# Block 0 of group 0 ahead of block 1's statistics, block 1's factors on GpSimd, and fewer dummy matmuls, in a fused state-space and MLP kernel

## The chip, the cores and the metric

The kernel runs on one core of a Trainium2 chip. The metric is the device time of one execution in microseconds (us). The kernel before took 154.12 us as the median of 3 runs (153.42 to 154.88). All times inside an execution are counted from the start of the profiled span.

## The reference, cut to what matters

One input x of 2048 tokens by 448 features is normalised, and two branches read the result: a linear recurrence over the tokens (A), and an MLP with a second normalisation (B). The output is x + A * silu(B).

```python
x = A_x
xn = _layernorm(x)
s = _A_ref(xn, ...)                    # h[t] = Lam_bar*h[t-1] + B_bar xn[t];  y = 2 Re(C h) + xn*Dskip
def _B_ref(x, w1, b1, w2, b2):
    y = _layernorm(x)
    h = _gelu(y @ w1 + b1)             # 448 -> 1792
    return h @ w2 + b2                 # 1792 -> 448
return x + s * _silu(_B_ref(xn, ...))
```

## The kernel before, in words

**Tiles.** The tokens are cut into four groups of 512, each group into two blocks (b = 0, 1) of 256, and each block into two halves (par = 0, 1: even and odd tokens) of 128. A half is one tile of 128 partitions by 448. For each group the MLP's first layer (mm1, L809) runs in seven steps j of two columns-of-128 each, every step in two phases: a first of 6 matmuls and a second of 8, then a GELU on ScalarE (L813). Then come the second layer (mm2, L836), and the recurrence's matmuls (L737, L879, L882).

**Order.** All work is a list of tasks. Each task names its engine and what it reads and writes, and the program adds semaphore waits for these dependences. The list ORDER (L162) gives the order in which tasks are issued, and so the order inside each engine's queue; SECOND (L181) lists the tasks that take the second of two possible engines. Every engine works strictly in its own order: what stands behind a waiting instruction waits too.

**The opening.** Group 0 starts differently from the others, because nothing is there yet. For block 0 each half is loaded on its own, for block 1 both halves come in one transfer. Per half there is a chain:

- `first_stats` (L424): BN_STATS and BN_AGGR on VectorE (L431, L432) give mean and variance, written `mv`; then the factor r1 = (var*(1+eps) + eps^2)^(-1/2). It is called r10, r12 for block 0's halves and r11, r13 for block 1's. It comes from ScalarE as Ln and Exp: for block 0 per half (L434, L435), for block 1 both halves together (L438, L439).
- `first_apply` (L447): VectorE writes the normalised half (L453; below `xm0p1`, `xm0p0`, `xm1p1`, `xm1p0` for block and half), TensorE transposes it in four pieces (L460), and ScalarE or VectorE copies the result to SBUF (L419; `xmT...`).
- mm1 of steps j = 0 to 4 for block 0 alone needs only block 0's two `xmT` tiles; j = 5, 6 run for both blocks, and j = 0 to 4 follow for block 1.

TensorE's order in the opening is: 26 dummy matmuls; `parameters` (L529, L530: five tiny matmuls that turn three parameter rows into columns); 12 dummies; transposes of xm0p1; 5 dummies; transposes of xm0p0; 5 dummies; `b1_columns` (L602, L603: six tiny matmuls that turn the bias b1 into columns, copied by L605 to `b1f`); 42 mm1 matmuls for j = 1, 2, 0 of block 0; the eight transposes of xm1p1 and xm1p0; then the other 126 mm1 matmuls, of which the first six are j = 4, the next 28 are j = 3, j = 4 and the first phase of j = 5, and the next 70 begin with j = 0 of block 1. A dummy (L422) multiplies the tile `ones`, which VectorE fills first (L309), into a bank that nobody reads.

Other tasks that matter below, all small: `ca` (L540, GpSimd) and `cr` (L541, ScalarE); `f2`, `f1`, `f4` on GpSimd (L534, L537, L552) and `f3` and a second `f2` on VectorE (L539, L538), where f4 reads f3; `iota` (L317, GpSimd); `ln_scale` (L478 to L482: five instructions on GpSimd, with a power in L480, that write all of group 0's factors again, among them the places of r10 to r13, so they must follow all readers of these); the three `wrap` instructions (L542 to L544, GpSimd) after it, and the Abs on ScalarE (L554) that reads their result. The table load for GELU (L443) is issued on ScalarE once cr and r10 to r13 are done. Copies of the upper 64 rows of w1 (L354, `w1c_0` to `w1c_3`, one for each chunk of w1) go on VectorE; a second phase of mm1 needs the copy of its chunk. The bias b1 comes in by two transfers that GpSimd issues (L363, L364).

Of the kernel before, what the change touches and what calls it, by code (L numbers as in the profile page):

```python
# [7 lines left out]
ACT = mybir.ActivationFunctionType  # L8
# [171 lines left out]
""".split()]  # L180
SECOND = [int(k) for k in """  # L181
46 54 55 62 64 67 70 75 77 84 108 113 131 134 159 161 163 164 166 178 185 186 188 190 191 221 223 225 227 229 231 239 249 250 259 267 269 332 363 365
366 385 401 402 437 448 469 481 483 488 492 500 502 503 505 511 529 530 610 613
# [8 lines left out]
LN_EPS = 1e-5  # L192
# [8 lines left out]
def bass_recurrent_scan__ssm_conv_s5__mixer_channel_mlp__prompt_kernel(  # L201
# [18 lines left out]
    with ExitStack() as es:  # L220
        def SB(name, shape, dtype=BF):
            return es.enter_context(nc.sbuf_tensor(name, shape, dtype))

        ident = SB("ident", [128, 128])
        ones = SB("ones", [128, 128])
# [80 lines left out]
        with nc.Block():  # L306

            S0 = -100
            dve(lambda e: e.memset(ones[:], 1.0), [], ["ones"])  # L309
# [110 lines left out]

            def dummies(n, rd=()):
                pe([lambda e: e.matmul(psum[:, 3, 0:128], ones[:, :], ones[:, :], start=True, stop=True) for _ in range(n)], ["ones", *rd], ["ps3"])  # L422

            def first_stats(b):  # L424

                for par in range(2):
                    q = 2 * par + b
                    var, mean = lnmv[:, 0, q, 1:2], lnmv[:, 0, q, 0:1]
                    r1, key = lnw[:, 0, 2, 1, q:q + 1], xk(0)[par:par + 1] if b == 0 else xk(1)
                    src, dst = x_all[:, b, par, :], xn2_sb[:, b, par * 512:par * 512 + D]  # L430
                    dve(lambda e, q=q, src=src: e.bn_stats(lnst[:, q, :], src), key, [f"st{q}"])  # L431
                    dve(lambda e, q=q: e.bn_aggr(lnmv[:, 0, q, :], lnst[:, q, :]), [f"st{q}"], [f"mv0_{q}"])  # L432
                    if b == 0:
                        kb.add("act", [lambda e, var=var, r1=r1: e.activation(r1, var, ACT.Ln, scale=1.0 + LN_EPS, bias=eps[:, 1:2]),  # L434
                                       lambda e, r1=r1: e.activation(r1, r1, ACT.Exp, scale=-0.5)], [f"mv0_{q}", "eps", "warm"], [f"r1{q}"], chain=True)  # L435
                    elif par == 1:
                        vs2, rs2 = lnmv[:, 0, 1:4:2, 1], lnw[:, 0, 2, 1, 1:4:2]
                        kb.add("act", [lambda e: e.activation(rs2, vs2, ACT.Ln, scale=1.0 + LN_EPS, bias=eps[:, 1:2]),  # L438
                                       lambda e: e.activation(rs2, rs2, ACT.Exp, scale=-0.5)], ["mv0_1", "mv0_3", "eps", "warm"], ["r11", "r13"], chain=True)  # L439

            def gelu_table():
                kb._sem("gelu0")
                kb.add("act", lambda e: e.preload_act_table_set("gelu_apprx_tanh_and_others"), ["cr", "r10", "r12"] + ["r11", "r13"] * (not 0), ["Wg0"], sem="gelu0")  # L443

            def first_apply(b):

                for par in range(2):  # L447
# [13 lines left out]
                    if b == 0:  # L461
                        if par == 0:
                            dummies(5, ["xm0p0"])
# [143 lines left out]

            def rows():

                for k, (dst, key, scale) in enumerate(((b2bc, "b2bc", 1.0), (dbc, "dbc", 0.5))):  # L610
                    bank, at = 6 - k, 64 + 32 * k
                    pe([lambda e, bank=bank, at=at: e.matmul(psum[:, bank, 0:D], ones[at:at + 1, :], vrows[at:at + 1, 64:512], start=True, stop=True)], ["ones", f"vr{3 + k}"], [f"ps{bank}"])
                    kb.either(("act", lambda e, bank=bank, dst=dst, scale=scale: e.activation(dst[:], psum[:, bank, 0:D], ACT.Copy, scale=scale)),
                              ("dve", lambda e, bank=bank, dst=dst, scale=scale: e.tensor_scalar(dst[:], psum[:, bank, 0:D], scale, None, op0=ALU.mult)), [f"ps{bank}"], [key])
# [309 lines left out]
            dummies(12 if 1 else 10, ["vr0"])  # L924
# [3 lines left out]
            dummies(5, ["st0"])  # L928
# [100 lines left out]
```

## Time and profile before

| what | value |
|---|---|
| median of 3 runs | 154.12 us (153.42 to 154.88) |
| the profiled execution's own time | 153.63 us |
| its span, first to last instruction | 151.9 us |
| TensorE (PE) busy | 147.6 us, 97% of the span, 1136 matmuls |
| VectorE (DVE), ScalarE (ACT), GpSimd (POOL) busy | 128.2, 98.4, 40.8 us |

The share of busy time says little about the opening, since TensorE counts as busy while it runs dummies. The opening is read from the rows in order of time, one engine after another. A row gives the start, the length, the engine, the line, the operation with what it writes and reads, the count of merged instructions and, in square brackets, how long the engine stood idle before and what ended that. "PEld" is the weight load that goes ahead of each matmul.

### The profile page before, as it was taken

What the parts mean: (1) busy time and instruction counts of PE and PEld (TensorE: products, weight loads), DVE (VectorE), ACT (ScalarE), POOL (GpSimd) and SP (SyncE); (2) the same over time, 40 slices, a digit from 0 to 9 for tenths busy, and PEclk for the clock granted to TensorE, in tenths of its full rate; (3) what the DMA queues carried; (4) which work ended last, traced back from release to release, by engine and by line L of the source; (5) the groups of instructions that cost most, each with busy time, mean ns of one, the idle gap of its engine ahead of it and who ended that gap; (6) DMA issues with size and microseconds to landing.
All of it is one profiled execution on the core that took longest, in us unless ns stands there. A gap on an engine that the chain in (4) does not pass through costs nothing.

```text
span 151.9 us, 2990 instructions
## 1 busy us (share of the span) xinstructions
PE 147.6 (97%) x1136; PEld 87.5 (58%) x1136; DVE 128.2 (84%) x270; ACT 98.4 (65%) x182; POOL 40.8 (27%) x100
## 2 busy tenths in 40 slices
PE   7999999999999999999999999999999999999992
PEld 7886755444566577545444556754444666555561
DVE  3978969899998969999999996379968727999984
ACT  3787998888789559997798610462579833067400
POOL 5377870053021910010366006200071040000200
PEclk9999999999999999999999999999999999999999
DMA  4999999889996100700003032610340001100022
GB/s 117 270 309 389 262 231 182 175 150 154 214 213 165 23 0 0 138 0 4 0 0 63 4 60 53 146 60 4 60 109 14 4 0 60 60 0 0 4 102 79
DMA packets 31236, 14.73 MB, mean 97 GB/s; under 512 B 24752, under 2 KB 30774, under 8 KB 31222
## 3 DMA queue, kind: packets, MB, share of 16 engines
q1 hardware_dynamic: 30912, 14.26, 41.9%
q0 software_dynamic: 160, 0.23, 0.6%
q8 instruction: 9, 0.15, 0.4%
q10 hardware_dynamic: 150, 0.05, 0.1%
q14 instruction: 5, 0.04, 0.1%
HBM read 6.89 MB, written 1.84 MB: 57 GB/s over the span
## 4 chain that ended last, share of the span: by engine, by line
PE 96%; DVE 2%; issue 0%; DVEq 0%
PE psum L809 29%; PE psum L836 28%; PE psum L737 14%; PE psum L879 12%; PE psum L882 4%; PE psum L422 3%; PE psum L720 3%; PE psum L885 1%; DVE t L893 1%; PE psum L460 1%; DVE tmp L899 1%; PE psum L705 1%; PE psum L602 0%; DVE ones L309 0%; PE psum L529 0%
## 5 line engine op out<-in xcount | busy, mean ns | idle before, releaser
L809 PE MATMUL psum<-xn2T,w_sb 64*128 64x512 bf16 (+1 forms) x462 | 44.6, 345 | 0.2
L836 PE MATMUL psum<-w_sb,gT 128*128 128x448 bf16 x224 | 44.4, 353 | 0.0
L813 ACT ACTIVATE gT<-psum,b1f 128x512 bf16<-128x512 f32 (+1 forms) x66 | 36.0, 625 | 10.6 <-PE psum L809 10.4
L809 PEld LDWEIGHTS psum<-xn2T,w_sb 64*128 64x128 bf16 x462 | 24.0, 109 | 19.7 <-ACT gT L813 2.3
L836 PEld LDWEIGHTS psum<-w_sb,gT 128*128 128x128 bf16 x224 | 21.6, 98 | 20.3 <-issue 0.6
L419 ACT ACTIVATE u_sb<-psum 128x512 bf16<-128x512 f32 (+2 forms) x22 | 10.5, 478 | 23.0 <-PE psum L737 22.7
L737 PE MATMUL psum<-xnT,BT 128*128 128x256 bf16 x196 | 24.0, 273 | 0.0
L737 PEld LDWEIGHTS psum<-xnT,BT 128*128 128x128 bf16 x196 | 18.9, 98 | 5.4 <-issue 1.1
L761 DVE TENSOR_TENSOR_SCAN s_w<-dk,vs 128x774 f32<-128x774 f32 x8 | 14.0, 1760 | 0.1
L899 POOL TENSOR_TENSOR tmp<-t,x_all 128x448 bf16<-128x448 bf16 x5 | 5.2, 1031 | 33.1 <-DVE t L896 30.7
L500 ACT ACTIVATE xn_sb<-x_all,lnw 128x448 bf16<-128x448 bf16 (+2 forms) x21 | 13.0, 661 | 1.2 <-DVE xn_sb L499 1.1
L419 ACT ACTIVATE vs<-s_w 64x256 bf16<-64x256 f32 (+2 forms) x16 | 10.9, 682 | 2.6 <-DVE s_w L761 1.5
L879 PE MATMUL psum<-CZ,h_sb 128*128 128x448 bf16 x56 | 11.9, 353 | 0.0
L839 DVE TENSOR_TENSOR o<-psum,b2bc 128x448 f32<-128x448 f32 x16 | 9.7, 614 | 1.7 <-PE psum L836 1.5
L879 PE MATMUL psum<-CQ,h_sb 128*128 128x448 bf16 (+2 forms) x54 | 10.5, 332 | 0.0
L879 PEld LDWEIGHTS psum<-CZ,h_sb 128*128 128x128 bf16 x56 | 5.4, 98 | 4.7 <-DVE lnmv L407 0.4
L401 DVE BATCH_NORM_STATS2 lnst<-x_all 128x6 f32<-128x448 bf16 x12 | 7.0, 614 | 0.6 <-DMA x_all<-in_A_x_dram 0.6
L879 PEld LDWEIGHTS psum<-CQ,h_sb 128*128 128x128 bf16 x54 | 5.1, 98 | 4.0 <-DVE t L893 0.4
L882 PE MATMUL psum<-M,xnT 128*128 128x448 bf16 x32 | 7.4, 352 | 0.0
L891 DVE TENSOR_TENSOR Cr<-psum,xd 128x448 f32<-128x448 f32 x7 | 4.3, 620 | 3.5 <-PE psum L885 3.4
L480 POOL TENSOR_TENSOR lnw<-lnw,mhalf 128x8 f32<-128x8 f32 x3 | 7.0, 2332 | 0.3
L499 DVE TENSOR_SCALAR xn_sb<-x_all,lnw 128x448 bf16<-128x448 bf16 (+2 forms) x19 | 6.9, 395 | 0.0
(160 smaller groups left out, 189.8 us busy)
## 6 DMA issues: line engine op xcount, KB each, us to landing
out_dram<-tmp SPq DMA_DIRECT2D x7, 224.0 KB, 2.0
x_all<-in_A_x_dram SPq DMA_DIRECT2D x3, 448.0 KB, 4.3
w_sb<-in_B_w_dram SPq DMA_DIRECT2D x3, 448.0 KB, 8.5
w_sb<-in_B_w_dram SPq DMA_DIRECT2D x3, 384.0 KB, 4.9
vs<-in_A_C_re_dram SPq DMA_DIRECT2D x1, 392.0 KB, 11.5
Bn<-in_A_B_im_dram SPq DMA_DIRECT2D x1, 336.0 KB, 10.4
Bn<-in_A_B_re_dram SPq DMA_DIRECT2D x1, 336.0 KB, 10.8
vs<-in_A_C_im_dram SPq DMA_DIRECT2D x1, 336.0 KB, 11.3
```

Of the source, the lines that this page charges most:

```text
L401: dve([lambda e, b=b, par=par, q=q: e.bn_stats(lnst[:, q, :], x_all[:, 2 * g + b, par, :])], [f"x{2 * g + b}"] , [f"st{q}"], 0.62, prio)
L419: kb.either(("act", [lambda e, o=o, i=i: e.activation(o, i, ACT.Copy) for o, i in pairs]), ("dve", [lambda e, o=o, i=i: e.tensor_copy(o, i ...
L480: power = fns + [lambda e: e.tensor_tensor(w(2), w(0), mhalf[:].to_broadcast([128, 2, nq]), ALU.pow), lambda e: e.tensor_tensor(w(3), mean ...
L500: ("act", [lambda e, o=o, i=i: e.activation(o, i, ACT.Identity, bias=nb, scale=rs) for o, i in parts], 0.75, 0.2)]
L737: fns = [lambda e, r=r, m=m, d=d: e.matmul(psum[:, 4, r * NK:(r + 1) * NK], BT[:, m, d, :], xnT[:, gx, d, :], start=(d == 0), stop=(d == 6 ...
L761: dve(lambda e, so=so, vi=vi: e.tensor_tensor_scan(so, dk[:].rearrange("p i c -> p (i c)"), vi, 0.0, ALU.mult, ALU.add), ["v", "vl", "dk", ...
L809: return lambda e: e.matmul(view(bk[k]), w1_sb[rows, d, fcol(2 * j + k)], rhs[rows, d, :, :], start=not second and n == 0, stop=second and ...
L813: act([lambda e, k=k: e.activation(gT[:, gb, 2 * j + k, :].rearrange("p (r c) -> p r c", r=2)[:, :, cols], view(bk[k]), ACT.Gelu_apprx_tan ...
L836: fns = [lambda e, fi=fi: e.matmul(psum[:, bk, 0:D], gT[:, gb, fi, q * 128:(q + 1) * 128], w2_sb[:, fi, :], start=(fi == 0), stop=(fi == N ...
L839: dve(lambda e: e.tensor_tensor(o2[:, fb, :], psum[:, bk, 0:D], b2bc[:], ALU.add), [f"ps{bk}", "b2bc"], [f"oo{fb}"], 0.62, prio - 76)
L879: fns = [lambda e, k=k: e.matmul(psum[:, bk, c0:c1], h_sb[:, hb, k, k0:k0 + 128], cm[:, k, c0:c1], start=(k == 0), stop=False) for k in ra ...
L882: fns += [lambda e, d=d: e.matmul(psum[:, bk, c0:c1], xnT[:, gx, d, xs], M0[:, d, c0:c1], start=False, stop=(d == 3)) for d in range(4)]
```

## The change

The diff, with ORDER and SECOND left out (they are renumbered, since the task that filled `ones` is gone):

```diff
-        ones = SB("ones", [128, 128])
...
-            dve(lambda e: e.memset(ones[:], 1.0), [], ["ones"])
...
+            one = nc.const_aps.tensor_like(1.0, ident[:])
+
             def dummies(n, rd=()):
-                pe([lambda e: e.matmul(psum[:, 3, 0:128], ones[:, :], ones[:, :], start=True, stop=True) for _ in range(n)], ["ones", *rd], ["ps3"])
+                pe([lambda e: e.matmul(psum[:, 3, 0:128], one, one, start=True, stop=True) for _ in range(n)], list(rd), ["ps3"])
...
-                        kb.add("act", [lambda e: e.activation(rs2, vs2, ACT.Ln, scale=1.0 + LN_EPS, bias=eps[:, 1:2]),
-                                       lambda e: e.activation(rs2, rs2, ACT.Exp, scale=-0.5)], ["mv0_1", "mv0_3", "eps", "warm"], ["r11", "r13"], chain=True)
+                        kb.add("pool", [lambda e: e.tensor_scalar(rs2, vs2, 1.0 + LN_EPS, LN_EPS * LN_EPS, op0=ALU.mult, op1=ALU.add),
+                                        lambda e: e.tensor_tensor(rs2, rs2, mhalf[:, 0, :].to_broadcast([128, 2]), ALU.pow)], ["mv0_1", "mv0_3", "mhalf"], ["r11", "r13"], chain=True)
...
-                kb.add("act", lambda e: e.preload_act_table_set("gelu_apprx_tanh_and_others"), ["cr", "r10", "r12"] + ["r11", "r13"] * (not 0), ["Wg0"], sem="gelu0")
+                kb.add("act", lambda e: e.preload_act_table_set("gelu_apprx_tanh_and_others"), ["cr", "r10", "r12"], ["Wg0"], sem="gelu0")
...
-                            dummies(5, ["xm0p0"])
+                            dummies(2, ["xm0p0"])
...
-            def rows():
...
-            dummies(12 if 1 else 10, ["vr0"])
+            dummies(9, ["vr0"])
...
-            dummies(5, ["st0"])
+            dummies(3, ["st0"])
```

`rows` was never called. The dummies now read a constant 1.0 that the runtime's preamble has already stored, one element for each partition, read 128 times over. Apart from the renumbering, ORDER and SECOND move these tasks, and no others:

| engine | order before | order after |
|---|---|---|
| TensorE | xm0p0's transposes, dummies, b1_columns, mm1 | xm0p0's transposes, b1_columns, dummies, mm1 |
| VectorE | ones, ..., xm0p1, stats of block 1 half 0, xm0p0, stats of half 1, both aggregates, copy xmT0p0, w1c_1, b1f, w1c_0, f3, f2, xm1p1, xm1p0 | ..., xm0p1, xm0p0, stats of block 1 half 0, copy xmT0p0, b1f, stats of half 1, both aggregates, w1c_0, f3, f2, xm1p1, xm1p0 |
| ScalarE | copy xmT0p1, cr, block 1's factors, table load | copy xmT0p1, cr, w1c_1, table load |
| GpSimd | ident, eps, eps, ident, b1 transfer 1, mhalf, b1 transfer 2, ca, iota, f2, ..., sgn, f1, f4, ln_scale, wrap | ident, b1 transfer 1, b1 transfer 2, ident, eps, eps, mhalf, ca, f2, f1, f4, iota, block 1's factors, ..., sgn, ln_scale, wrap |

The order of transfers on SyncE's queue is the same.

More of the change, by code (lines that the diff above doesn't have):

```diff
@@ L162 @@
 ORDER = [int(k) for k in """
[17 rows of a table removed]
[17 rows of a table added]
 """.split()]
 SECOND = [int(k) for k in """
-46 54 55 62 64 67 70 75 77 84 108 113 131 134 159 161 163 164 166 178 185 186 188 190 191 221 223 225 227 229 231 239 249 250 259 267 269 332 363 365
-366 385 401 402 437 448 469 481 483 488 492 500 502 503 505 511 529 530 610 613
+28 45 53 54 61 63 66 69 74 76 83 107 112 130 133 158 160 162 163 165 177 184 185 187 189 190 220 222 224 226 228 230 238 248 249 258 266 268 331 362
+364 365 384 400 401 436 447 468 480 482 487 491 499 501 502 504 510 528 529 609 612
 """.split()]
@@ L606, in b1_columns @@
                           ["ps4"], ["b1f"])
-            def rows():
[L610 to L614, printed above, removed]
             def skips():
```

34 rows, old and new, of the table ORDER are left out of this document.

## The prediction

> **What bounds the kernel now.** I read the busy times by stretch first, then the chain that ended last, then the rows in order of time of each engine from 1 to 17 us.
>
> ```profile
> PE 147.6 (97%) x1136; PEld 87.5 (58%) x1136; DVE 128.2 (84%) x270; ACT 98.4 (65%) x182; POOL 40.8 (27%) x100
> ...
> 12.50:19.40 6.90, 6.77 (x95) 4.66 (x94) 6.52 (x26) 6.27 (x14) 5.35 (x19) 1.00 1.09 311
> 19.40:147.50 128.10, 128.10 (x881) 71.88 (x882) 111.25 (x211) 83.89 (x149) 28.45 (x57) 1.00 0.36 71
> ```
>
> The columns of the last two are the stretch, its length, then busy time and count of PE, PEld, DVE, ACT, POOL. From 19.40 to 147.50 TensorE is busy in 128.10 of 128.10 us. So what the change makes earlier or later up to 19.4 us, it makes so for the end. TensorE's own rows of the opening:
>
> ```profile
> 1.11 2.95 PE L422 MATMUL psum<-ones 128*128 128x128 bf16 x26 [1.11 <-DVE ones L309]
> ...
> 4.30 1.46 PE L422 MATMUL psum<-ones 128*128 128x128 bf16 x12
> 5.56 0.50 PE L460 MATMUL psum<-ident,xn_sb 128*128 128x128 bf16 x4
> 5.89 0.44 PE L422 MATMUL psum<-ones 128*128 128x128 bf16 x5
> 6.17 0.39 PE L460 MATMUL psum<-ident,xn_sb 128*128 128x128 bf16 x4
> ...
> 7.17 2.48 PE L809 MATMUL psum<-xn2T,w_sb 64*128 64x256 bf16 x42
> 9.58 0.62 PE L460 MATMUL psum<-ident,xn_sb 128*128 128x128 bf16 x8
> 10.14 9.25 PE L809 MATMUL psum<-xn2T,w_sb 64*128 64x256 bf16 x126
> ...
> 10.58 1.57 PEld L809 LDWEIGHTS psum<-xn2T,w_sb 64*128 64x128 bf16 x28 [0.20 <-ACT gT L813]
> 12.47 4.94 PEld L809 LDWEIGHTS psum<-xn2T,w_sb 64*128 64x128 bf16 x70 [0.32 <-ACT gT L813]
> ```
>
> Real work starts at 7.17. The 12 dummies run to 5.56, and the transposes of block 0 stand behind them; block 1's transposes are at 9.58, directly behind the 42 matmuls, without a wait. The two waits for ACT show that GELU is nearly as binding here as TensorE. VectorE's and ScalarE's rows:
>
> ```profile
> 4.44 0.40 DVE L453 TENSOR_SCALAR xn_sb<-x_all,lnmv,lnw 128x448 bf16<-128x448 bf16 x1
> ...
> 5.58 0.62 DVE L431 BATCH_NORM_STATS2 lnst<-x_all 128x6 f32<-128x448 bf16 x1
> 6.12 0.30 DVE L432 BATCH_NORM_AGGREGATE lnmv<-lnst 128x2 f32<-128x6 f32 x2
> 6.60 0.42 DVE L419 COPY xn2T<-psum 128x512 bf16<-128x512 bf16 x1 [0.17 <-PE psum L460]
> 7.05 0.29 DVE L354 COPY w_sb<-w_sb 64x512 bf16<-64x512 bf16 x1
> 7.26 0.16 DVE L605 COPY b1f<-psum 128x14 f32<-128x14 f32 x1
> 7.34 0.22 DVE L354 COPY w_sb<-w_sb 64x256 bf16<-64x256 bf16 x1
> 7.59 0.17 DVE L539 TENSOR_SCALAR ang<-ang 128x4 f32<-128x4 f32 x1
> ...
> 7.74 0.70 DVE L453 TENSOR_SCALAR xn_sb<-x_all,lnmv,lnw 128x448 bf16<-128x448 bf16 x2
> 9.31 0.31 DVE L354 COPY w_sb<-w_sb 64x512 bf16<-64x512 bf16 x1 [0.88 <-DMA w_sb<-in_B_w_dram]
> ...
> 10.19 0.75 DVE L419 COPY xn2T<-psum 128x512 bf16<-128x512 bf16 x2
> ...
> 4.88 0.20 ACT L435 ACTIVATE lnw<-lnw 128x1 f32<-128x1 f32 x1
> ...
> 6.09 0.60 ACT L419 ACTIVATE xn2T<-psum 128x512 bf16<-128x512 bf16 x1 [0.70 <-PE psum L460]
> ...
> 7.28 1.28 ACT L443 ACT_TABLE_LOAD   x1
> 8.65 0.84 ACT L813 ACTIVATE gT<-psum,b1f 128x256 bf16<-128x256 f32 x2
> 9.69 1.57 ACT L813 ACTIVATE gT<-psum,b1f 128x256 bf16<-128x256 f32 x4 [0.20 <-PE psum L809]
> ...
> 13.03 0.23 ACT L554 ACTIVATE ang<-ang 128x16 f32<-128x16 f32 x1
> 13.89 3.94 ACT L813 ACTIVATE gT<-psum,b1f 128x512 bf16<-128x512 f32 x8 [0.63 <-PE psum L809]
> ```
>
> Block 1 is normalised at 7.74 to 8.44, so it has 1.1 us in hand before TensorE asks for it at 9.58. This slack is what the change spends.
>
> **The change, part by part.**
>
> *The fill of `ones` and the first dummies.* VectorE's fill, for which TensorE waited until 1.11, goes, and the 26 dummies start up to 0.25 us sooner (an estimate: VectorE's fill and its hand-over). Parameters behind them may still wait for their rows' transfer. I take no gain here; if nothing else holds them, all up to 5.56 moves by 0.25. A repeated element as operand is in no row: between nothing and 0.05 us for each of 14 dummies, 0.7 in all; the first 26 hide theirs. I take nothing, since the operand has the same shape. `rows` was never called: nothing.
>
> *Fewer dummies.* The 12 start (1.46 - 0.31)/11 = 0.105 apart, 0.31 being the length of one. Nine end at 4.30 + 9 x 0.105 = 5.25, 0.31 sooner. xm0p1 is ready (4.44 + 0.40 = 4.84). xm0p0 now follows it at once: r10 is ready at 4.88 + 0.20 = 5.08, so it runs 5.11 to 5.49. The four transposes take 0.42 at that pace, to 5.67, the three dummies to 5.89 (later ones stand 0.056 apart), and xm0p0's transposes begin at 5.89 instead of 6.17. Before, the copy began 0.43 after that and mm1 0.57 after the copy: now the copy is at 6.32 and mm1 at 6.89, 0.28 sooner. VectorE is free for it: block 1's first statistics end at 5.40 + 0.62 = 6.02. b1_columns come ahead of the last dummies; their transfers are issued earlier on GpSimd, past eps and ident; these are first wanted by block 0's factors and by parameters, which stand right ahead of the 12 dummies of 4.30, so I cost this at nothing (if it held parameters, all would move with them one for one).
>
> *ScalarE.* Its two small operations for block 1 go, w1c_1 comes in (0.6 by the row of the same width at 6.09, against 0.29 on VectorE). Copy of xmT0p1 at 5.88 to 6.48, cr, w1c_1 to about 7.1, table load 7.12 instead of 7.28, first GELU 8.49 instead of 8.65. mm1 wants w1c_1 after twelve matmuls, at 7.6: covered. The third pair's GELU follows TensorE: 9.41 instead of 9.69.
>
> *Block 1's statistics, now behind block 0.* From the copy at 6.32, by the spacings of the rows: b1f +0.45 (6.60 to 7.05) at 6.77; statistics of half 1 +0.08 at 6.85; both aggregates done +0.84 (5.58 to 6.42) at 7.69. Before it was 6.42. Then w1c_0 at 7.61, and f3 +0.25 at 7.86, done 8.03.
>
> *The factors on GpSimd.* Its rows:
>
> ```profile
> 5.68 0.34 POOL L317 IOTA dk<- 128x256 f32 x1
> 6.12 0.23 POOL L534 TENSOR_SCALAR cw<-cw 128x4 f32<-128x4 f32 x1
> ...
> 7.85 0.39 POOL L552 TENSOR_SCALAR ang<-ang 128x8 f32<-128x8 f32 x1 [1.14 <-DVE cw L538]
> 8.72 0.20 POOL L478 TENSOR_SCALAR lnw<-lnmv 128x4 f32<-128x4 f32 x1 [0.48 <-ACT L443]
> 9.00 0.19 POOL L479 TENSOR_SCALAR lnw<-lnmv 128x4 f32<-128x4 f32 x1
> 9.28 1.68 POOL L480 TENSOR_TENSOR lnw<-lnw,mhalf 128x8 f32<-128x8 f32 x1
> ...
> 12.47 0.22 POOL L544 TENSOR_TENSOR ang<-ang 128x16 f32<-128x16 f32 x1
> ```
>
> In the new order f4 and iota stand ahead of the factors, and f4 waits for f3 on VectorE. That is the new wait: f4 starts 0.09 after f3 (7.76 to 7.85), at 8.12 to 8.51; iota at 8.46; the next instruction 0.44 after it (5.68 to 6.12) at 8.90; the power 0.28 later (8.72 to 9.00) at 9.18. Its price for 2 columns is not in the trace: between 0.19 (a plain instruction) and 1.68 (the power of 8 columns, if it is all fixed cost). I take 0.19 fixed plus 2/8 of the other 1.49, 0.57, since a power that costs far more than a plain instruction of the same tile should go with its elements. So the factors are there at 9.75, against about 7.2 before.
>
> *Who waits.* VectorE waits at xm1p1 until 9.84; xm1p1 and xm1p0 take 0.70, to 10.54, and w1c_2, two table instructions and the copies of block 1's transposes (10.19 before) stand behind. TensorE is through its 42 at 6.89 + 2.48 = 9.37, and waits: first transposes at 10.28, the second four at 10.58, each 0.28 long, done 10.86. The next six mm1 matmuls start there, against 10.14: 0.72 late, the 0.28 won included. The 28 after them start at 11.19, against 10.58 (there ACT held them by 0.20): 0.61 late. They need the copies of block 1 only for their last six, at 12.3, when VectorE has done them (about 12.2). So 70 matmuls start at 13.08 against 12.47: 0.61 late.
>
> *ln_scale and the Abs.* ln_scale overwrites the factors, so it waits for xm1p0: 10.63 instead of 8.72, 1.91 late. The wrap ended at 12.69 and now ends at 14.60; the Abs stands on ScalarE ahead of the GELU of 13.89, which then starts at 14.88. TensorE would let it start at 13.89 + 0.61 = 14.50: it is 0.38 late. Its cover:
>
> ```profile
> 15.83 1.63 ACT L813 ACTIVATE gT<-psum,b1f 128x512 bf16<-128x512 f32 x3
> ...
> 15.74 1.48 PE L809 MATMUL psum<-xn2T,w_sb 64*128 64x256 bf16 x24
> ```
>
> The fifth GELU begins at 15.83, so the fourth frees its bank there; TensorE, at 15.74, comes to that bank after six matmuls of 0.055, at 16.07. With some 0.1 for the semaphore this leaves 0.15. So TensorE loses 0.38 - 0.15 = 0.23 more. The b2 transfer on GpSimd's queue moves behind ln_scale too; its first reader stands behind the first mm2, so I cost it at nothing (without that cover it would add 1.91 at most).
>
> *Sum.* 0.61 + 0.23 = 0.84 us later at 19.4, and so at the end. The profiled execution took 153.63 (span 151.9 and 1.73 around it): 154.47. The median shown is 0.49 above that execution, which makes it 154.96, say 155.0.
>
> **The rivals.**
>
> *ScalarE sets the pace, and the opening's gain stays (the other side).* If the factors come in time, the GELU that runs 0.28 sooner pulls everything: 154.12 - 0.28 = 153.8. It decides at the factors' time: the six matmuls must be done when GELU frees their bank at 10.2, so block 1's transposes by 9.9 and the factors by 8.8. For it: TensorE waited for ACT twice, and if the first dummies start 0.25 sooner, all moves by that, and the power may cost 0.19. Against it: both together bring 9.75 to 9.12 only; f4's wait for f3 would have to shorten too.
>
> *The power has a fixed cost.* At 1.68 for 2 columns everything behind it is 1.11 later: 0.84 + 1.11 = 1.95, 156.1. For it: other instructions on GpSimd cost nearly the same for 4 and for 8 columns (0.23 and 0.39). Against: only the power is so dear.
>
> *TensorE stays slow.* The dummies stand 0.105 apart up to 5.56 and 0.056 after 5.89, though the clock column shows 1.00 throughout; full pace came some 4.6 us after the first matmul. With idle stretches in the opening it may come later. If it came another 4.6 us later, at 10.3, the 42 matmuls would do in 3.4 us what takes 1.7, and end at 11.1; the wait for block 1 hides most of it, and 0.8 remains: 155.8. Against: it came while dummies, parameters and transposes were mixed, and of 48 dummies 40 remain.
>
> [...]
>
> **How the numbers follow.** Forecast 0.55; ScalarE's pace 0.18; power with fixed cost 0.15; slow TensorE 0.08; something else 0.04. The range takes in the case on the other side with the scatter of runs (153.5) and the dear power (156.2). The likeliest case alone spans 154.4 (power 0.19, and half of the Abs) to 155.7 (operands of dummies dear, ln_scale's power longer). A measurement of this kernel tells about 1% from no change: 152.6 and 155.7 are the bounds. Slower by over 1%: 0.15, half of the slow case, and 0.08 of the forecast's upper end, 0.27. Faster by over 1% has no mechanism here, since the opening has at most 0.5 us to give: 0.04. Within 1%: 0.69.
>
> **What would show it.** Right: mm1's first row at about 6.9; f4 on GpSimd ending its wait for f3 near 8.1; the power at 9.2 and about 0.6 long; a gap of TensorE of some 0.9 ahead of block 1's transposes; the Abs ahead of a GELU near 14.9; mm2 starting 0.8 after 19.32. Wrong: block 1's transposes directly behind the 42 matmuls (then the time falls), the power at over 1 us, 42 matmuls that take 4 us, or a start of mm2 that is later while the end is not.

## The result, and the profile after

| | median | shortest to longest | executions |
|---|---|---|---|
| before, in this comparison | 153.77 us | 153.3 to 154.88 | 4 |
| changed | 155.75 us | 155.41 to 156.22 | 4 |

The ratio is 1.0128, with a 95% interval from 1.0089 to 1.0166. The changed kernel is slower, by 1.98 us; 0.84 was forecast, and slower by over 1% had a chance of 0.27. A ratio, here and below, leaves out executions over 1.5% above the kernel's fastest: 1 of 12 in two of the experiments and 4 of 11 in the last one. Its profiled execution took 155.45 us, with a span of 153.7, 1.8 longer than before's 151.9. TensorE's rows of it first (start, length, engine, line, operation; the bracket is idle time ahead of the row and what ended it). mm1 is line 801 now and mm2 line 828:

```profile
4.20 0.70 PE L422 MATMUL psum<-const-bfloat16-1.0 128*128 128x128 bf16 x9
5.29 0.40 PE L460 MATMUL psum<-ident,xn_sb 128*128 128x128 bf16 x4 [0.40 <-DVE xn_sb L453]
...
7.06 4.12 PE L801 MATMUL psum<-xn2T,w_sb 64*128 64x256 bf16 x42
11.12 0.62 PE L460 MATMUL psum<-ident,xn_sb 128*128 128x128 bf16 x8
...
20.86 1.31 PE L828 MATMUL psum<-w_sb,gT 128*128 128x448 bf16 x6
```

mm2 starts at 20.86 against 19.32, so 1.54 of the 1.8 us are lost by then. But there is no wait ahead of block 1's eight transposes. Instead the 42 matmuls of block 0 took 4.12 us; before they took 2.48. The stretches show why (stretch, length, busy time and count of PE, PEld, DVE, ACT, POOL, then the granted clock of TensorE, the DMA share and GB/s):

```profile
5.80:7.20 1.40, 1.10 (x16) 0.78 (x16) 1.40 (x5) 1.15 (x4) 0.63 (x3) 0.95 0.85 219
7.20:10.20 3.00, 3.00 (x30) 2.55 (x29) 1.25 (x7) 2.16 (x4) 1.68 (x6) 0.50 1.05 307
10.20:12.50 2.30, 2.30 (x38) 1.74 (x34) 2.21 (x8) 1.34 (x5) 1.63 (x3) 0.94 1.06 362
```

The granted clock is 0.50 from 7.20 to 10.20. Finer stretches of the same profile read 1.00 up to 7.06, 0.54 from 7.06 to 7.20, 0.50 from 10.20 to 10.48 and 0.98 from 10.48 to 10.60, so the half clock lasted from about 7.06 to 10.48. That is the rival "TensorE stays slow", in another form: the dummies had reached full pace (nine in 0.70 from 4.20), and then the granted clock fell to 0.50. TensorE's longest stop before that, 0.40 us ahead of 5.29, came of a late transfer: VectorE waited 0.54 us for the second half of block 0, as it does in neither of the two later profiles of this kernel.

```profile
4.11 0.63 DVE L431 BATCH_NORM_STATS2 lnst<-x_all 128x6 f32<-128x448 bf16 x1 [0.54 <-DMA x_all<-in_A_x_dram]
```

Whether this stop let the clock fall was not tested. The new chain on GpSimd is there too, but block 1 was ready before TensorE asked:

```profile
8.24 0.24 POOL L552 TENSOR_SCALAR ang<-ang 128x8 f32<-128x8 f32 x1 [1.52 <-DVE cw L538]
8.44 0.35 POOL L315 IOTA dk<- 128x256 f32 x1
8.87 0.19 POOL L438 TENSOR_SCALAR lnw<-lnmv 128x2 f32<-128x2 f32 x1
9.14 0.73 POOL L439 TENSOR_TENSOR lnw<-lnw,mhalf 128x2 f32<-128x2 f32 x1
```

f4 (L552) waits 1.52 us for f3, which stands right ahead of the L538 that the row names; iota and the factors stand behind it, as forecast. The power takes 0.73. One execution thus shows a wait that is hidden and a clock that is not the usual one. It could not say what the change costs typically, nor through what. So the changed kernel was profiled again, twice.

### The profile page after: what moved, and what is told of

Its sections match the earlier page's. It is cut to its first block, busy times and chain, and to the rows that moved or that the text cites. A ratio compares the mean times of both kernels' runs of the same rounds, so it can differ in the third digit from the quotient of the medians.

```text
span 153.7 us, 2974 instructions
## 1 busy us (share of the span) xinstructions
PE 148.6 (97%) x1128; PEld 87.6 (57%) x1128; DVE 128.3 (83%) x268; ACT 98.6 (64%) x181; POOL 41.9 (27%) x102
## 3 DMA queue, kind: packets, MB, share of 16 engines
HBM read 6.89 MB, written 1.84 MB: 57 GB/s over the span
## 4 chain that ended last, share of the span: by engine, by line
PE 89%; DVE 3%; ACT 3%; DMA 2%; issue 1%; SPq 0%; DVEq 0%; ACTq 0%
PE psum L828 28%; PE psum L801 26%; PE psum L729 14%; PE psum L871 12%; PE psum L874 4%; PE psum L712 3%; DMA x_all<-in_A_x_dram 2%; ACT gT L805 2%; PE psum L877 1%; ACT L618 1%; DVE t L885 1%; DVE lnst L431 1%; DVE tmp L891 1%; PE psum L697 1%; DVE o L831 0%
## 5 line engine op out<-in xcount | busy, mean ns | idle before, releaser
L801 PE MATMUL psum<-xn2T,w_sb 64*128 64x512 bf16 (+1 forms) x462 | 46.2, 355 | 0.6 <-ACT gT L805 0.3
L801 PEld LDWEIGHTS psum<-xn2T,w_sb 64*128 64x128 bf16 x462 | 25.2, 112 | 20.7 <-ACT gT L805 2.9
L480 POOL TENSOR_TENSOR lnw<-lnw,mhalf 128x8 f32<-128x8 f32 x3 | 7.0, 2332 | 0.3
```

Source lines behind the costliest of these rows:

```text
L801: return lambda e: e.matmul(view(bk[k]), w1_sb[rows, d, fcol(2 * j + k)], rhs[rows, d, :, :], start=not second and n == 0, stop=second and ...
```

## The experiments

The theory to be tested is the prediction's: the factors come late on GpSimd, and TensorE waits for block 1. The first rival is the clock, that is, too few dummies. Each run is compared with before, run on the same chip; the number behind a time is the ratio to it with its 95% interval.

### The changed kernel again, unchanged, twice

> The changed kernel once more, unchanged, for more executions beside a second profile. Theory F (block 1's factors are late because they stand behind f4's wait for f3): TensorE waits some 0.7 to 1.0 us ahead of block 1's transposes when its pace is full, and the time is 1.0 to 1.5 above the kernel before, in every execution. Theory C (half clock decides): the 42 matmuls take about 4.1 us again and the transposes stand directly behind them; in executions without the half clock the time is near that of the kernel before, so the times fall into two groups 1.5 us apart.

It took 154.69 us (1.0066, 1.0045 to 1.0088), 0.92 above before, a little less than was expected of the wait; one execution of nine (155.87) lies apart. This is TensorE in its profiled execution (154.44, span 152.6), in three stretches of time:

```profile
6.62 2.50 PE L801 MATMUL psum<-xn2T,w_sb 64*128 64x256 bf16 x42
9.94 0.70 PE L460 MATMUL psum<-ident,xn_sb 128*128 128x128 bf16 x8 [0.82 <-DVE xn_sb L453]
10.57 2.63 PE L801 MATMUL psum<-xn2T,w_sb 64*128 64x256 bf16 x38
...
19.73 2.44 PE L828 MATMUL psum<-w_sb,gT 128*128 128x448 bf16 x12
...
30.43 5.36 PE L801 MATMUL psum<-xn2T,w_sb 64*128 64x512 bf16 x48
36.09 4.12 PE L801 MATMUL psum<-xn2T,w_sb 64*128 64x512 bf16 x36 [0.30 <-ACT gT L805]
```

At full pace the 42 matmuls end at 9.12 and TensorE waits 0.82 us for VectorE's xn_sb. This is the forecast's gap. VectorE in turn waits for the factors, which GpSimd has done at 8.72 + 0.73 = 9.45:

```profile
8.72 0.73 POOL L439 TENSOR_TENSOR lnw<-lnw,mhalf 128x2 f32<-128x2 f32 x1
9.48 0.70 DVE L453 TENSOR_SCALAR xn_sb<-x_all,lnmv,lnw 128x448 bf16<-128x448 bf16 x2 [1.70 <-POOL lnw L439]
```

A third measurement asked which of the first two is the usual one:

> The changed kernel, unchanged. Theory (wait, gap at the table load, and half the clock in some executions): near 154.7, and a median over 155.3 only if the 42 matmuls of block 0 take over 3 us in its profile. Rival (the first measurement's 155.75 is the typical one, the second's 154.69 was not): 155.5 or more with the 42 at 2.5.

154.69 us again (1.0073, 1.0044 to 1.0102), with the 42 matmuls in 2.50 and a wait of 0.69. So the usual cost of the change is 0.9 to 1.0 us, and the wait is in both of these profiles. Of all 22 executions of the changed kernel 7 took over 155.2 us: all 4 of the first measurement, 1 of 9 and 2 of 9 of the others.

### The dummies put back

```diff
-                            dummies(2, ["xm0p0"])
+                            dummies(5, ["xm0p0"])
-            dummies(9, ["vr0"])
+            dummies(12, ["vr0"])
-            dummies(3, ["st0"])
+            dummies(5, ["st0"])
```

> The changed kernel with 12, 5 and 5 dummies again instead of 9, 3 and 2; all else as changed. Theory A (the clock: idle stretches of TensorE in the opening let it fall to half pace from about 7 to 10 us): the 42 matmuls take 2.5 us instead of 4.1, and block 1's transposes then wait for their factors until about 10.4 instead of starting at 11.1, so the time falls by about 0.7 us against the changed kernel, to about 155.0, and stays 1.2 above the kernel before. Theory B (the factors alone): no change against the changed kernel, 155.7. If the slow pace came by chance of the run and not of the dummies, the mean does not move either.

154.66 us (1.0064, 1.0039 to 1.009), the same as the changed kernel's usual time. That is below both forecasts, which took the first measurement's 155.75 for the usual time. More dummies don't bring the loss back, so the usual loss isn't the clock. Its profiled execution was its longest (155.59) and shows a cost that I had put at nothing:

```profile
10.71 0.70 PE L460 MATMUL psum<-ident,xn_sb 128*128 128x128 bf16 x8 [0.65 <-DVE xn_sb L453]
...
28.92 2.82 PE L828 MATMUL psum<-w_sb,gT 128*128 128x448 bf16 x14 [0.31 <-DVE o L831]
```

Here mm1 began at 7.56, so everything behind it was later. The b2 transfer, issued at 15.83, took 8.5 us to land (7.4 from 15.07 in the changed kernel's second profile), and TensorE waited 0.31 us for `o`, which wants b2.

### Block 1's factors ahead of f4 and iota

One task is moved up in ORDER: 101 are the factors, 65 is iota.

```diff
-28 30 100 114 23 54 57 5 101 65 32 53 ...
+28 30 100 101 114 23 54 57 5 65 32 53 ...
```

> The changed kernel with block 1's factors ahead of f4 and iota on GpSimd, so that they no longer wait for f3 on VectorE. Theory A: block 1 is ready at about 9.6 instead of 10.6, but TensorE is at half pace until about 10 and comes to the transposes at 11.1 anyway; gain at the opening 0, and at most 0.3 later through ln_scale and the b2 transfer, which move up by 1 us: 155.4 to 155.7. Theory B: the transposes follow at 9.6 and the time falls by 0.9 or more, to 154.8 or less.

153.71 us (0.9992, 0.997 to 1.0013): with this one move the loss is gone. The factors wait for their own statistics only, and TensorE for nothing ahead of block 1's transposes (GpSimd's rows, then TensorE's):

```profile
7.27 0.22 POOL L438 TENSOR_SCALAR lnw<-lnmv 128x2 f32<-128x2 f32 x1 [1.07 <-DVE lnmv L432]
7.57 0.73 POOL L439 TENSOR_TENSOR lnw<-lnw,mhalf 128x2 f32<-128x2 f32 x1
```

```profile
6.54 2.50 PE L801 MATMUL psum<-xn2T,w_sb 64*128 64x256 bf16 x42
8.98 0.62 PE L460 MATMUL psum<-ident,xn_sb 128*128 128x128 bf16 x8
...
35.26 4.77 PE L801 MATMUL psum<-xn2T,w_sb 64*128 64x512 bf16 x42 [0.29 <-ACT gT L805]
```

That shows the theory: it is the place behind f4's wait that costs, not the engine on which the power runs. But mm2 starts at 18.91, 0.41 before before's 19.32, while the span (151.8) is only 0.1 shorter. Some 0.3 is given back, in the last row's wait near 35, which before doesn't have. It comes from ScalarE, behind the last silu (L833):

```profile
30.44 0.58 ACT L833 ACTIVATE g_sb<-o 128x448 bf16<-128x448 f32 x1 [0.59 <-DVE o L831]
31.41 1.28 ACT L618 ACT_TABLE_LOAD   x1 [0.39 <-ACT g_sb L833]
```

The same two rows of before:

```profile
30.85 0.58 ACT L841 ACTIVATE g_sb<-o 128x448 bf16<-128x448 f32 x1 [1.04 <-DVE o L839]
31.51 1.28 ACT L626 ACT_TABLE_LOAD   x1
```

The table load for group 1's GELU came 0.08 us after the silu's end before, and comes 0.39 after it now. Every profile of the changed kernel has this, on ScalarE and on TensorE.

### Only the dummies, and both undone

> The kernel before with 9, 3 and 2 dummies instead of 12, 5 and 5; nothing else. Theory A: the pace falls here too, the 42 matmuls take up to 1.6 us longer, and the time rises by 1 to 1.6 us, to 154.8 to 155.4. Theory B: fewer dummies only bring mm1 forward, by 0.1 to 0.3 us: 153.5 to 153.8.

The kernel before with 9, 3 and 2 dummies: 153.6 us (0.9991, 0.997 to 1.0011). In its profile mm1 starts at 6.82 instead of 7.17, the 42 matmuls take 2.62 us, and the granted clock is 1.00 throughout from 4.00 to 19.40. Fewer dummies alone neither cost nor bring anything that this measurement can tell.

> The changed kernel with 12, 5 and 5 dummies and with the factors ahead of f4 and iota. Theory A: with full pace and the factors at about 8.8, mm1 starts near 7.2 and nothing waits long: within 0.3 us of the kernel before, 153.5 to 154.1. Theory B: the same as with the factors ahead alone, 154.8 or less, since dummies play no part.

The changed kernel with the dummies put back and the factors moved: 153.84 us (1.0015, 0.9994 to 1.0036). Again no loss. The dummies put back alone took 154.66 on the same chip; the two kernels differ in the one move, which is thus worth 0.82.

### The factors on ScalarE

```diff
-                        kb.add("pool", [lambda e: e.tensor_scalar(rs2, vs2, 1.0 + LN_EPS, LN_EPS * LN_EPS, op0=ALU.mult, op1=ALU.add),
-                                        lambda e: e.tensor_tensor(rs2, rs2, mhalf[:, 0, :].to_broadcast([128, 2]), ALU.pow)], ["mv0_1", "mv0_3", "mhalf"], ["r11", "r13"], chain=True)
+                        kb.add("act", [lambda e: e.activation(rs2, vs2, ACT.Ln, scale=1.0 + LN_EPS, bias=eps[:, 1:2]),
+                                       lambda e: e.activation(rs2, rs2, ACT.Exp, scale=-0.5)], ["mv0_1", "mv0_3", "eps", "warm"], ["r11", "r13"], chain=True)
```

> The changed kernel with block 1's factors on ScalarE as Ln and Exp again, ahead of the table load in ScalarE's order; all else as changed. Theory F: block 1's transposes follow the 42 matmuls without a wait (factors at about 8.3), but the table load now ends near 9.6 and the third pair's GELU near 11.3, so TensorE waits there instead and the 70 matmuls start about 0.8 us later than in the kernel before: 154.6 to 155.0, and the move to GpSimd is worth something only if the wait for f3 goes. Theory C: no difference to the changed kernel, 155.7.

154.11 us (1.0024, 1.0008 to 1.004). The wait ahead of the transposes goes; they start at 9.21. But the factors hold the table load, which now begins at 8.00, and TensorE waits behind the transposes instead:

```profile
9.21 0.62 PE L460 MATMUL psum<-ident,xn_sb 128*128 128x128 bf16 x8
10.36 2.82 PE L801 MATMUL psum<-xn2T,w_sb 64*128 64x256 bf16 x36 [0.53 <-ACT gT L805]
```

mm2 starts at 19.74, as late as in the changed kernel's second profile (19.73): with the statistics behind block 0's normalising, the factors cost the opening as much on ScalarE as on GpSimd behind f4. Only the place ahead of f4 made the move off ScalarE worth while (18.91 there). The time is below the expected 154.6 to 155.0: the 70 matmuls start 0.42 later than before (12.89), not 0.8, and the loss at the second table load is missing. That load stands 0.07 behind its silu here, without the gap. The page of the changed kernel counts 181 instructions on ScalarE:

```profile
PE 148.6 (97%) x1128; PEld 87.6 (57%) x1128; DVE 128.3 (83%) x268; ACT 98.6 (64%) x181; POOL 41.9 (27%) x102
```

The page of before has 182, and that of this kernel 183. That made a theory of the 0.3: it hangs on the place of the table load in ScalarE's stream of instructions.

### One more instruction on ScalarE

A copy of 128x1 into a spare tile, behind the first table load, which nothing reads:

```diff
-            act(lambda e: e.preload_act_table_set("natural_log_exp_and_others"), [], ["warm"], 0.05, 5 * PINNED, "exp")
+            act([lambda e: e.preload_act_table_set("natural_log_exp_and_others"), lambda e: e.activation(spare[:], nc.const_aps.tensor_like(1.0, spare[:]), ACT.Copy)], [], ["warm"], 0.05, 5 * PINNED, "exp")
```

First together with the moved factors:

> The changed kernel with the factors ahead of f4 and iota, and one small spare ScalarE copy (128x1) right behind the first table load, whose result nobody reads. It puts every later ScalarE instruction one place further in the stream, where it stood in the kernel before. Theory P (the 0.39 us ahead of the second GELU table load, 0.08 in the kernel before, hangs on the place in ScalarE's instruction stream): the gap is 0.08 again, TensorE does not wait for GELU ahead of group 1's third pair, and the time falls by 0.3 us against the factors ahead alone, to about 153.4. Theory Q (it hangs on when the last silu is done): the gap stays 0.39, 153.7.

153.35 us (0.9986, 0.9957 to 1.0016), the shortest median of all, though the interval takes in no change. The gap is gone, on ScalarE and on TensorE:

```profile
30.45 0.58 ACT L834 ACTIVATE g_sb<-o 128x448 bf16<-128x448 f32 x1 [0.63 <-DVE o L832]
31.11 1.28 ACT L619 ACT_TABLE_LOAD   x1
```

```profile
29.62 10.11 PE L802 MATMUL psum<-xn2T,w_sb 64*128 64x512 bf16 x90
```

The span is 151.5, 0.4 below before's, which is what mm2 gains here. Then the copy alone, in the changed kernel:

> The changed kernel, with one spare copy of 128x1 on ScalarE behind its first table load, so that ScalarE's stream has as many instructions as before (169). Theory (0.3 us of the change's loss hangs on the place of the second GELU table load in that stream): the load stands some 0.08 behind the silu again, TensorE has no gap near 36, and the time is 0.3 below the changed kernel's beside it, about 154.4, while the wait ahead of block 1's transposes stays at 0.8. Rival (the gap belongs to the later opening, or to the factors' place): the load still stands 0.39 behind the silu and the time stays.

154.49 us (1.0051, 1.0025 to 1.0076), beside 154.69 (1.0073) for the changed kernel on the same chip; the intervals overlap. The profile is plainer than the time:

```profile
31.61 0.58 ACT L834 ACTIVATE g_sb<-o 128x448 bf16<-128x448 f32 x1 [1.04 <-DVE o L832]
32.26 1.28 ACT L619 ACT_TABLE_LOAD   x1
```

The gap is gone, with the factors where the change put them. In this execution mm2 started 0.42 later than in the changed kernel's beside it (20.08 against 19.66), and the span is only 0.1 longer (152.6 against 152.5): the 0.3 came back. So an instruction that does nothing useful removes the gap in both orders, and the gap belongs to the changed stream, not to the late factors.

### The power replaced, and the power twice

Two kernels change the price on the disputed path. The first replaces the power by a plain multiplication, so block 1's factors are not those of the reference:

```diff
-lambda e: e.tensor_tensor(rs2, rs2, mhalf[:, 0, :].to_broadcast([128, 2]), ALU.pow)]
+lambda e: e.tensor_tensor(rs2, rs2, mhalf[:, 0, :].to_broadcast([128, 2]), ALU.mult)]
```

> The changed kernel with the power of block 1's two factors replaced by a plain multiplication (the factors are then not those of the reference; work left out: the power). Theory (the power's 0.73 stands on the path to block 1's transposes): the factors come 0.54 sooner, TensorE's wait ahead of the transposes falls from 0.82 to about 0.28, and the time falls by 0.3 to 0.5 against the changed kernel beside it. Rival (the factors wait for something behind GpSimd): wait and time stay.

154.22 us (1.0036, 1.0014 to 1.0059), 0.47 below the changed kernel beside it, though the intervals of the two ratios overlap. GpSimd and TensorE:

```profile
8.91 0.20 POOL L439 TENSOR_TENSOR lnw<-lnw,mhalf 128x2 f32<-128x2 f32 x1
```

```profile
9.60 0.70 PE L460 MATMUL psum<-ident,xn_sb 128*128 128x128 bf16 x8 [0.28 <-DVE xn_sb L453]
```

The wait is 0.28, as expected. But in this execution mm2 starts no sooner than in the changed kernel's beside it (19.65 against 19.66): what was won is lost again in a stop of TensorE's weight loads for which the profile names no releaser and which the other profile doesn't have.

```profile
18.29 0.48 PEld L801 LDWEIGHTS psum<-xn2T,w_sb 64*128 64x128 bf16 x10 [0.31 <-issue]
```

So for the gain in time the medians alone speak. The second works the power out twice, first into a spare tile:

```diff
+                                        lambda e: e.tensor_tensor(spare[:], rs2, mhalf[:, 0, :].to_broadcast([128, 2]), ALU.pow),
```

> The changed kernel, with the power of block 1's two factors worked out twice, first into a spare tile. Theory (the power stands on TensorE's path): its wait ahead of block 1's transposes grows from 0.7-0.8 by a power's 0.73 to about 1.5, and the time by 0.6 to 0.75, to a median of about 155.3. Beside it, on the share of long executions (7 of 22 of the changed kernel took over 155.2, half a microsecond above its usual 154.7): if the longer idle stretch of TensorE is what lets the clock fall afterwards, over half of the executions now lie another 1 to 1.6 higher, near 156.5 to 157, and a profile of such a one shows matmuls 0.1 apart behind the transposes of block 1. If the long executions have to do with the transfers of the start, their share stays at a quarter or a third.

155.64 us (1.0144, 1.0121 to 1.0167), 155.55 to 155.93 in four executions. TensorE's rows:

```profile
6.49 2.50 PE L803 MATMUL psum<-xn2T,w_sb 64*128 64x256 bf16 x42
10.58 0.70 PE L462 MATMUL psum<-ident,xn_sb 128*128 128x128 bf16 x8 [1.59 <-DVE xn_sb L455]
11.22 9.21 PE L803 MATMUL psum<-xn2T,w_sb 64*128 64x256 bf16 x126
20.36 1.88 PE L830 MATMUL psum<-w_sb,gT 128*128 128x448 bf16 x9
...
28.91 2.82 PE L830 MATMUL psum<-w_sb,gT 128*128 128x448 bf16 x14 [0.43 <-DVE o L833]
```

The wait is 1.59, and mm2 is later than in the changed kernel by 20.36 - 19.66 = 0.70. With the power at 0.20, 0.73 and two of about 0.7, the wait is 0.28, 0.69 to 0.82 and 1.59: the power stands in full on the path to block 1's transposes. And 126 matmuls in 9.21 behind an idle stretch of 1.59 us show that here this stretch didn't make the clock fall (the granted clock is 1.00 from 4.00 to 19.40); nor did any of the four executions come out at 156.5 to 157. The median is longer than expected by the wait of 0.43 at 28.91, b2 again. The transfer's line in three kernels, with the microseconds from issue to landing last; before:

```profile
b2bc<-in_B_b_dram POOLq DMA_DIRECT2D x1, 112.0 KB, 6.8
```

The changed kernel in its first profile:

```profile
b2bc<-in_B_b_dram POOLq DMA_DIRECT2D x1, 112.0 KB, 8.3
```

And with two powers, with the row on VectorE that reads it:

```profile
b2bc<-in_B_b_dram POOLq DMA_DIRECT2D x1, 112.0 KB, 8.6
```

```profile
24.36 0.62 DVE L833 TENSOR_TENSOR o<-psum,b2bc 128x448 f32<-128x448 f32 x1 [1.91 <-DMA b2bc<-in_B_b_dram]
```

GpSimd issued it at 13.58, 15.51 and 15.70, so it landed near 20.4, 23.8 and 24.3. Count from mm2's start to VectorE's first row that reads b2. TensorE waited for nothing at 2.93 us (the changed kernel, 23.79 - 20.86) and near 3.40 (the plain multiplication: b2 issued at 14.75 and 8.3 to land, so 23.05 - 19.65), but 0.31 at 3.87 (the dummies put back, 24.36 - 20.49) and 0.43 at 4.00 (two powers, 24.36 - 20.36). The cover ends about 3.6 us behind mm2's start, an estimate from these four.

### Hardly any dummies

The kernel with the factors ahead, and 1, 1 and 1 dummies in the place of 9, 3 and 2:

> The changed kernel with the factors ahead of f4 and iota and with 1, 1 and 1 dummies behind parameters instead of 9, 3 and 2. Theory C (idle stretches in the opening cost the clock): TensorE is at half pace during the 42 matmuls in most executions, which then take up to 4.6 us instead of 2.5, and the time rises by 1 to 2 us against the factors ahead alone, to 154.7 to 155.7. If the clock does not hang on these dummies: mm1 starts at the same time or up to 0.3 sooner, 153.4 to 153.8.

155.26 us (1.0079, 1.0053 to 1.0106), from 153.65 to 156.25. TensorE in its profile:

```profile
4.01 0.29 PE L422 MATMUL psum<-const-bfloat16-1.0 128*128 128x128 bf16 x1
5.11 0.61 PE L460 MATMUL psum<-ident,xn_sb 128*128 128x128 bf16 x4 [0.81 <-DVE xn_sb L453]
...
7.09 3.67 PE L801 MATMUL psum<-xn2T,w_sb 64*128 64x256 bf16 x42
10.69 0.62 PE L460 MATMUL psum<-ident,xn_sb 128*128 128x128 bf16 x8
```

With TensorE idle for 0.81 us at 4.3 the 42 matmuls take 3.67, about one and a half times the usual 2.50, and no wait behind them hides it, since block 1 is early. So the dummies do hold the pace. Moving the factors cures the wait, not the pace; with 9, 3 and 2 dummies the same order kept it in the profile (42 in 2.50), and all 12 executions took 153.53 to 154.25.

## Why the prediction was right or wrong

**The main step was right, and it was shown.** The factors' place behind f4 and iota makes TensorE wait ahead of block 1's transposes: 0.82 us in the second profile, 0.91 by the prediction (9.37 to 10.28). Moving the factors alone takes the wait and the loss away, and a dearer power lengthens it.

**That the sum came near the usual loss is in part luck: its terms were off both ways.** Against the second profile of the changed kernel:

| term | predicted | measured |
|---|---|---|
| start of mm1 | 6.89 | 6.62 |
| f4 on GpSimd | 8.12 | 7.80 |
| power of 2 columns | 0.57 | 0.73 |
| factors there | 9.75 | 9.45 |
| first matmuls behind the transposes, later by | 0.72 | 10.57 - 10.14 = 0.43 |
| matmuls behind the first 34, later by | 0.61 | 12.80 - 12.47 = 0.33 |
| what the Abs adds | 0.23 | 0.41 - 0.33 = 0.08 |
| start of mm2, later by | 0.84 | 19.73 - 19.32 = 0.41 |
| TensorE's wait behind the second GELU table load | none | 0.30 |
| span, later by | 0.84 | 152.6 - 151.9 = 0.7 |

The two executions at the usual pace that have a profile took 154.44 and 154.28, both below their medians of 154.69. So the table accounts for 0.7 of the usual 0.9 to 1.0, and the rest isn't traced.

The start was mis-sized: I took no gain from the dummies' operand that needs no fill. TensorE's first row, the 26 dummies, starts at 0.83 instead of 1.11, and the parameters behind them at 3.70 instead of 4.00. The price of the repeated operand, between nothing and 0.05 us for each dummy, was my guess; the 26 took 2.93 us with it and 2.95 before. The 0.28 won at the start run through f3, f4 and the factors up to the transposes, and make most of the difference between 0.72 and 0.43. The power, 0.73 between the bounds of 0.19 and 1.68, went nearer to the plain instruction, as I had argued; 1.66 for 8 columns (L480 in the second profile) and 0.73 for 2 (L439) give 0.155 for each column and 0.42 fixed, an estimate from these two rows.

The Abs works as forecast, at a third of the price. It waits for GpSimd's wrap, GELU stands behind it (at 14.33, against the 14.88 worked out), and TensorE's weights wait for that GELU (PEld's rows of the second profile; before, they had 70 in one row from 12.47):

```profile
12.80 3.38 PEld L801 LDWEIGHTS psum<-xn2T,w_sb 64*128 64x128 bf16 x42 [0.32 <-ACT gT L805]
16.36 1.46 PEld L801 LDWEIGHTS psum<-xn2T,w_sb 64*128 64x128 bf16 x28 [0.18 <-ACT gT L805]
```

The 0.1 for the semaphore in the cover of the Abs was my guess, and no run shows it: in the kernel before, the two weight loads that waited for a GELU began 0.05 us after one ended (10.53 to 10.58 and 12.42 to 12.47).

**What the prediction missed is the 0.3 at the table load.** The step that failed is "So what the change makes earlier or later up to 19.4 us, it makes so for the end." One instruction fewer on ScalarE made TensorE wait 0.30 us at 36 us. The prediction's own sign for this ("a start of mm2 that is later while the end is not") was for the other direction.

**"I cost this at nothing", of b2, was a matter of how late.** It holds in the three profiles of the changed kernel, and failed by 0.31 with the dummies put back and by 0.43 with two powers, where the transfer took 8.5 and 8.6 us to land and not the 6.8 of before. It should have stood with the time at which the cover ends.

**The rivals.** ScalarE's pace is out, as TensorE waits for VectorE. The power with all its cost fixed is out (0.73); the argument for it, that 0.23 and 0.39 us are nearly the same, was a loose reading, though the row of 0.39 took 0.24 in the changed kernel. "TensorE stays slow" was true of the first profiled execution, in another form (it had full pace and lost it), where it gave 155.45 against the 155.8 worked out for it; the half clock hid the wait, as the prediction said it would. It is not the usual way: the matmuls of block 0 took 2.50 in the second and third profile. So the first median, 1.98 above before, lies above the usual 0.9 to 1.0, and the forecast of 0.84 is near the latter.

**What stays open** is what made 7 of 22 executions of the changed kernel longer than 155.2. Four of them are the whole first measurement, of which nothing on record says why. Only one of the seven has a profile, the one with half the clock. Its granted clock over the whole span is 0.989; the other six have 0.997 to 1.0, so by this column they didn't share its fall, but the column isn't a complete sign (below). Nor does the fall need late factors: an execution with the factors ahead and the spare copy has 0.989 too, and is the longest of its ten (155.0 against a median of 153.35).

Long executions aren't the changed kernel's alone either. More than 1 us above their own median are 3 of the 18 in its second and third measurement, 3 of 46 of four kernels with the same 9, 3 and 2 dummies but early factors (the dummies alone changed, the factors ahead, these with the spare copy, the factors on ScalarE), and 3 of 95 of the kernel before. That is a hint at the late factors and no more. The four executions with two powers speak against the longer idle stretch as such, and b2 behind its cover was argued for one execution, not shown for these.

## What to carry to other kernels

When work is moved to another engine, look at its place in that engine's queue: here the place behind an instruction that waits cost 0.8 us more than the one ahead of it. After a change, a second profile is worth having where the first shows a resource in an unusual state, since one execution's cause may not be the usual one. And a cover ("its reader comes later") should be written down with the time at which it ends.

## What the runs showed of the hardware

- The second GELU table load on ScalarE stood 0.38 to 0.39 us behind the instruction ahead of it in every profile of the changed stream, and 0.07 to 0.08 in the kernels that had one or two instructions more ahead of it. For the wait the profile names nothing but that instruction, which had ended. That the place in the stream decides was shown by an added copy, in two orders; why it does so is open.
- The half clock in the first profile lasted from about 7.06 to 10.48 by the granted clock (0.50 from 7.20 to 10.48, 0.98 right behind), that is 3.4 us. What let it fall these runs don't tell: an idle stretch of 1.59 us between matmuls (two powers) let the clock stand (1.00 on both sides, and 126 matmuls in 9.21 behind it), and in the first profile it fell behind gaps of at most 0.40 among dummies, parameters and transposes.
- The granted clock doesn't show all of it. In the kernel with hardly any dummies the clock column has 1.00 for the stretch in which the matmuls ran slow:

```profile
7.20:10.20 3.00, 3.00 (x36) 2.63 (x35) 2.25 (x10) 1.95 (x3) 2.14 (x8) 1.00 1.08 309
```

TensorE is busy throughout and does 36 matmuls in 3.00 us, 0.083 each, against 42 in 2.50 at full pace. Here the length of equal rows is the better sign.
